# Dealing the rows of a weight matrix to partitions in groups of four, and reading the other matrix's columns with a step of four

## The chip, the cores and the metric

The kernel runs on one core of a Trainium2 chip. The metric is the device time of one execution in microseconds (us). TensorE (PE in the profile, with PEld for its weight loads), VectorE (DVE), ScalarE (ACT), GpSimd (POOL) and the DMA engines work beside each other and wait for one another through semaphores.

## The reference

A gated linear attention (4 batches, 8 heads, 768 positions, head size 48) is followed by one feed-forward block over all 3072 tokens, whose activation is a rational function:

```python
state = f[:, :, t, :, None] * state + einsum('bhd,bhe->bhde', k[:, :, t], v[:, :, t])   # f = sigmoid(f_logit)
y[:, :, t] = einsum('bhd,bhde->bhe', q[:, :, t], state)
...
x = y.transpose(0, 2, 1, 3).reshape(3072, 384)
h = x @ w_in                                   # w_in 384 x 2048
P = a[0] + a[1]*h + a[2]*h**2 + a[3]*h**3
Q = 1.0 + abs(b[0])*abs(h) + abs(b[1])*h**2
out = (P / (Q + 1e-06)) @ w_out                # w_out 2048 x 384
```

All inputs and the output are float32. The hidden dimension of 2048 is an inner one: w_in makes its columns, w_out sums over its rows, and nothing else depends on the order in which its 2048 elements are kept.

## The kernel before, in words

The 3072 tokens are worked off in 12 units of 256 tokens (one batch and 256 positions each). A unit has an attention part, which ends in `xT`, the 384 features of its 256 tokens in bf16, three blocks of 128 on the partitions, and a feed-forward part. The 2048 hidden elements are cut into 16 tiles of 128, which lie on the partitions. Both weight matrices stay in SBUF in bf16 for the whole run: `w_in_sb` is 128 partitions x 3 feature blocks x 2048 columns, `w_out_sb` is 128 partitions x 16 hidden tiles x 384 columns.

The steps that matter here:

- `wi m0 m1` (L199) loads the columns of w_in for the hidden tiles m0 to m1, `wo m0 m1` (L205) the rows of w_out for them. Each is called four times with four tiles at a time. They are issued on GpSimd's DMA queue and convert float32 to bf16 on the way.
- `h n m0 m1` (L454) makes the hidden tiles m0 to m1 of unit n: for each tile three matmuls, one per feature block, with 128 columns of `w_in_sb` as the weights that are loaded into the array and the 256 columns of `xT` streamed past them, into the PSUM tile `hp`. `ha` and `hb` (L478) do the same for one group of unit 0 in two halves. Together they are 12 units x 16 tiles x 3 = 576 matmuls, each with a weight load of its own, in 48 groups of four tiles.
- `hy` (ACT, L484) copies `hp` to bf16. `sq`, `ab`, `p1`, `p2`, `pm`, `tv`, `gm` on DVE, `ln`, `lz`, `ex` on ACT, `u` on PE (L505) and the adding DMAs `zd` and `ta` on POOL (L519, L549) make the activation `gall` from it.
- `o n j m0 m1` (L567) sums the output of 128 tokens over the hidden tiles: `gall` is the loaded weight, the 384 columns of a tile of `w_out_sb` are streamed, into `op`. There are 384 of these matmuls. `oe` copies `op` out of PSUM, `so` stores it.
- On the attention side, `T` (L320) transposes, `sc` (L345) makes scores, `yb` and `yi` (L367) outputs, `kv` (L414, L420) and `si` (L425) states, `vm` (POOL, L360) copies part of v.

The order of all of these is a table written out by hand (`ORDER`); each engine carries out its own steps in that order and waits only for data and for buffers. Four PSUM slots pass between the PE steps. In the table the steps on w_out stand as follows:

```
... xa 3 0; wo 8 12; ...            wo 12 16; dz 1 @2; h 2 8 12 @2
... vm 3 1; wo 4 8; hy 2 8 12; wo 0 4; ...
o 0 1 8 12 @2; ...  o 0 0 8 12; ... o 0 1 12 16; ... o 0 1 4 8; ... o 0 1 0 4; ...
```

Of the kernel before, what the change touches and what calls it, by code (L numbers as in the profile page):

```python
# [100 lines left out]
def _at(t, dims, off=0):  # L101

    return bass.AP(tensor=t.tensor, offset=t.offset + off, ap=[t.ap[0]] + [list(d) for d in dims])
# [3 lines left out]
def kernel(  # L107
# [12 lines left out]
    nc = tc.nc  # L120
    B, H, S, D = q.shape
    C = 128
    P = 128
# [8 lines left out]
    R = C // 2  # L132
    E = 64
    W = 2 * D

    nc.scalar.preload_act_table_set("natural_log_exp_and_others")

# [19 lines left out]
    vmp = [consts.tile([P, 2, HP, 48], BF16, name=f"vmp{i}") for i in range(2)]  # L157
    states = [[consts.tile([P, HP, W], BF16, name=f"state{b}_{j}") for j in range(UB)] for b in range(B)]
    a_sb = consts.tile([P, 4], F32, name="a_sb")
# [5 lines left out]
    w_in_sb = consts.tile([P, KD, d_ff], BF16, name="w_in_sb")  # L165
    w_out_sb = consts.tile([P, KF, DM], BF16, name="w_out_sb")
# [5 lines left out]
    def unit(n):  # L172
        if n not in units:
            c, b = divmod(n, B)
            units[n] = dict(c=c, b=b, qk=qkp[n % 2], ls=lsp[n % 2], vm=vmp[n % 2], st=states[b])
        return units[n]

    def slot(i, shape, dtype, name):
        return slots[i].tile(shape, dtype, name=name, tag="s")
# [22 lines left out]
            behind(i, hold[1:])  # L202

    def load_w_out(m0, m1, hold=None):
        i = nc.gpsimd.dma_start(out=w_out_sb[:, m0:m1, :],  # L205
                            in_=moe_w_out[m0 * P:m1 * P, :].rearrange("(ko ki) n -> ki ko n", ki=P))
        if hold is not None:
            behind(i, hold[1:])

# [21 lines left out]
    def const_z(i):  # L231
        if i < 2:
            nc.vector.memset(lsp[i][:, :, :, D:E], 0.0)
            nc.vector.memset(qkp[i].rearrange("p i x h d -> p (i x h) d")[:, :, D:E], 0.0)
            nc.vector.memset(vmp[i][:, :, :, 16:32], 0.0)
        elif i == 2:
            nc.vector.memset(ind, 0.0)
            for j in range(UB):
                nc.vector.memset(ind[R * j:R * j + R, j:j + 1], 1.0)
        else:  # L240
            for b in range(B):
                nc.vector.memset(states[b][0].rearrange("p a d -> p (a d)").bitcast(F32), 0.0)
# [155 lines left out]
    def sv_open(n, sl):  # L398
        s = unit(n)
        if "sv" not in s:  # L400
            t = s["svt"] = slot(sl, [P, UB, 512], F32, "sv")
            s["sv"] = t[:, :, 0:HP * W].rearrange("p j (a e) -> p j a e", a=HP)
            s["al"] = t[:, 0, 448:448 + 2 * HP].rearrange("p (a j) -> p a j", j=UB)
# [39 lines left out]
    def st(n, j):  # L443
        s = unit(n)
        return nc.vector.tensor_mul(s["st"][1 - j], s["sv"][:, j], _at(s["ae"], [[UB, HP], [0, W]], j))

    def h(n, m0, m1, sl):
        s = unit(n)  # L450
        t = s["hp", m0] = slot(sl, [P, 4, NT], F32, "hp")
        for m in range(m0, m1):
            for kk in range(KD):
                nc.tensor.matmul(t[:, m - m0, :], w_in_sb[:, kk, m * P:(m + 1) * P],  # L454
                                 s["x"][:, kk].rearrange("p i j t -> p (i j t)"),
                                 start=(kk == 0), stop=(kk == KD - 1))

# [8 lines left out]
    def ha(n, m0, m1, sl):  # L466
        s = unit(n)
        s["hp", m0] = slot(sl, [P, 4, NT], F32, "hp")
        hk(n, m0, m1, 0)

    def hb(n, m0, m1):
        for kk in range(1, KD):
            hk(n, m0, m1, kk)

    def hk(n, m0, m1, kk):
        s = unit(n)
        for m in range(m0, m1):
            nc.tensor.matmul(s["hp", m0][:, m - m0, :], w_in_sb[:, kk, m * P:(m + 1) * P],  # L478
                             s["x"][:, kk].rearrange("p i j t -> p (i j t)"),
                             start=(kk == 0 and (m - m0) % 2 == 0), stop=(kk == KD - 1), skip_group_check=True)  # L480

# [100 lines left out]
    def behind(i, mark):  # L582
        tc.add_manual_dep(i.ins, marks[mark].ins.name,
                          mybir.DependencyInfo(mybir.DependencyClass.Sync, mybir.DependencyReason.DATA),
                          reason="begins behind it")

    steps = dict(ld=load, wi=load_w_in, wo=load_w_out, ab_=load_ab, cu=const_u, ci=const_i, cm=const_m,
                 cz=const_z, fa=coef_a, fb=coef_b, fr=coef_r, ef=ef, ls=ls, cs=cs, A=A, xa=xa, T=T, Te=Te,
                 sc=sc, mk=mk, vm=vm, yi=yi, yb=yb, kv=kv, si=si, ye=ye, ae=ae, st=st, h=h, ha=ha, hb=hb, hy=hy, sq=sq, ab=ab, u=u, ln=ln,
                 zv=zv, zd=zd, sa=sa, lz=lz, ex=ex, p1=p1, p2=p2, pm=pm, ta=ta, tv=tv, gm=gm, o=o, oe=oe, so=store, dz=dz)  # L590
    for step in ORDER.replace("\n", ";").split(";"):
# [34 lines left out]
```

## Time and profile before

| | |
|---|---|
| Time, median of 3 runs | 216.9 us (216.26 to 217.07) |
| Span of the profiled execution | 214.4 us |
| Median less span | 2.5 us |
| Busy: PE / DVE / ACT / POOL | 201.0 / 201.7 / 195.8 / 83.7 us |
| Granted TensorE clock | 1.000 |
| DMA | 43.20 MB in 61199 packets, mean 202 GB/s |

The span runs from the first to the last instruction of the execution that the profiler recorded. That execution's time outside the profiler is not listed beside it, so the 2.5 us around the span are taken from the median of the runs. [...] "Idle before" is the time an engine stood still ahead of an instruction, with what ended it.

### The profile page before, as it was taken

What the parts mean: (1) busy time and instruction counts of PE and PEld (TensorE: products, weight loads), DVE (VectorE), ACT (ScalarE), POOL (GpSimd) and SP (SyncE); (2) the same over time, 40 slices, a digit from 0 to 9 for tenths busy, and PEclk for the clock granted to TensorE, in tenths of its full rate; (3) what the DMA queues carried; (4) which work ended last, traced back from release to release, by engine and by line L of the source; (5) the groups of instructions that cost most, each with busy time, mean ns of one, the idle gap of its engine ahead of it and who ended that gap; (6) DMA issues with size and microseconds to landing.
All of it is one profiled execution on the core that took longest, in us unless ns stands there. A gap on an engine that the chain in (4) does not pass through costs nothing.

```text
span 214.4 us, 7128 instructions
## 1 busy us (share of the span) xinstructions
PE 201.0 (94%) x3166; PEld 139.9 (65%) x3166; DVE 201.7 (94%) x213; ACT 195.8 (91%) x204; POOL 83.7 (39%) x93
## 2 busy tenths in 40 slices
PE   5875999899999999999999899999999999999993
PEld 1544587567767686586687587686577676776461
DVE  4786899999999999999999999999999999999991
ACT  3574689999999999999999999999999999999990
POOL 5161009009165072183270496696350603114200
PEclk9999999999999999999999999999999999999999
DMA  5999999999999999999999499999499896988823
GB/s 143 240 257 217 201 242 197 195 223 223 187 200 248 247 235 219 253 228 203 192 292 193 81 294 215 209 225 208 89 192 200 164 196 126 174 282 151 187 84 148
DMA packets 61199, 43.20 MB, mean 202 GB/s; under 512 B 51184, under 2 KB 55024, under 8 KB 61168
## 3 DMA queue, kind: packets, MB, share of 16 engines
q0 software_dynamic: 21520, 23.86, 67.3%
q1 hardware_dynamic: 39360, 18.68, 34.5%
q8 instruction: 25, 0.41, 0.8%
q10 hardware_dynamic: 288, 0.20, 0.3%
q14 instruction: 6, 0.05, 0.1%
HBM read 25.17 MB, written 4.72 MB: 139 GB/s over the span
## 4 chain that ended last, share of the span: by engine, by line
PE 39%; DVE 29%; ACT 14%; DMA 9%; issue 6%; SPq 2%; POOL 1%; DVEq 0%
PE hp L454 13%; PE op L567 12%; DVE gall L557 6%; DMA w_in_sb<-in_moe_w_in_dram 6%; DVE gall L545 4%; ACT qi L527 4%; ACT hy L484 4%; DVE z L497 3%; DVE h L489 3%; DVE scm L353 3%; DMA fn<-in_f_logit_dram 3%; PE u L505 3%; DVE gall L531 3%; PE y L367 2%; DVE hy L536 2%
## 5 line engine op out<-in xcount | busy, mean ns | idle before, releaser
L567 PE MATMUL op<-w_out_sb,gall 128*128 128x384 bf16 x384 | 69.2, 326 | 0.4 <-DVE gall L557 0.4
L454 PE MATMUL hp<-xT,w_in_sb 128*128 128x256 bf16 x564 | 66.7, 273 | 2.1 <-DMA w_in_sb<-in_moe_w_in_dram 2.0
L454 PEld LDWEIGHTS <-w_in_sb 128*128 128x128 bf16 x564 | 54.2, 98 | 11.5 <-DMA w_in_sb<-in_moe_w_in_dram 2.5
L567 PEld LDWEIGHTS <-gall 128*128 128x128 bf16 x384 | 36.1, 98 | 23.6 <-DVE gall L557 0.8
L484 ACT CAST hy<-hp 128x1024 bf16<-128x1024 f32 x47 | 48.1, 1076 | 2.3 <-PE hp L478 1.4
L527 ACT ACTIVATE qi<-lq 128x2048 bf16<-128x2048 f32 (+1 forms) x26 | 48.0, 1861 | 0.1
L360 POOL COPY vmp<-vn 128x128 bf16<-128x128 bf16 x24 | 35.2, 1516 | 28.4 <-DMA vn<-in_v_dram 22.7
L549 POOL DMA_DIRECT2D gall<-hy x20 | 20.0, 1068 | 53.9 <-ACT lsp L276 10.6
L523 ACT ACTIVATE lq<-z 128x2048 f32<-128x2048 bf16 (+1 forms) x20 | 36.8, 1874 | 0.0
L353 DVE TENSOR_TENSOR scm<-sc,mask 128x1024 bf16<-128x1024 f32 x24 | 29.0, 1215 | 1.9 <-PE sc L345 1.7
L489 DVE TENSOR_TENSOR h<-hy 128x4096 bf16<-128x4096 bf16 (+2 forms) x19 | 28.5, 1500 | 0.0
L557 DVE TENSOR_TENSOR gall<-gall,qi 128x4096 bf16<-128x4096 bf16 (+2 forms) x17 | 28.2, 1666 | 0.2
L545 DVE TENSOR_TENSOR gall<-gall,h 128x4096 bf16<-128x4096 bf16 (+2 forms) x17 | 28.1, 1652 | 0.0
L519 POOL DMA_DIRECT2D z<-h x17 | 19.3, 1366 | 17.0 <-PE u L505 6.0
L302 ACT ACTIVATE A<-cs 128x768 f32<-128x768 f32 (+1 forms) x26 | 19.4, 799 | 1.8 <-PE cs L286 1.8
L193 POOL DMA_DIRECT2D vn<-in_v_dram x12 | 12.4, 1030 | 15.7 <-PE y L367 7.9
L531 DVE TENSOR_SCALAR gall<-hy,a_sb 128x4096 bf16<-128x4096 bf16 (+1 forms) x14 | 16.9, 1208 | 0.0
L536 DVE TENSOR_SCALAR hy<-hy,a_sb 128x4096 bf16<-128x4096 bf16 (+1 forms) x14 | 16.6, 1185 | 0.0
L497 DVE TENSOR_SCALAR z<-hy 128x4096 uint16<-128x4096 uint16 (+2 forms) x19 | 15.7, 834 | 0.4 <-ACT hy L484 0.4
L330 ACT COPY qkT<-tp 128x1024 f32<-128x1024 f32 x11 | 11.6, 1058 | 3.2 <-PE tp L320 3.2
L320 PE MATMUL tp<-ident,qkp 128*128 128x128 bf16 x192 | 12.9, 219 | 0.8 <-DVE qkp L308 0.5
L320 PEld LDWEIGHTS <-qkp 128*128 128x128 bf16 x192 | 11.5, 98 | 2.5 <-DVE qkp L308 0.9
(73 smaller groups left out, 255.8 us busy)
## 6 DMA issues: line engine op xcount, KB each, us to landing
gall<-hy POOLq DMA_DIRECT2D x18, 512.0 KB, 7.1
z<-h POOLq DMA_DIRECT2D x15, 512.0 KB, 8.4
fn<-in_f_logit_dram SPq DMA_DIRECT2D x11, 384.0 KB, 8.5
kn<-in_k_dram SPq DMA_DIRECT2D x11, 384.0 KB, 12.1
qn<-in_q_dram SPq DMA_DIRECT2D x11, 384.0 KB, 11.3
out_dram<-osb SPq DMA_DIRECT2D x11, 384.0 KB, 5.1
vn<-in_v_dram POOLq DMA_DIRECT2D x12, 192.0 KB, 8.9
w_in_sb<-in_moe_w_in_dram POOLq DMA_DIRECT2D x4, 384.0 KB, 10.1
```

The source lines that it names most:

```text
L320: nc.tensor.transpose(t[:, x, i, p, :], s["qk"][:, i, x, 2 * p:2 * p + 2, :].rearrange("t h d -> t (h d)"), ident)
L353: return nc.vector.tensor_mul(t, s["sc", g].rearrange("s r a i t -> s (r a) (i t)"), mb)
L360: nc.gpsimd.tensor_copy(s["vm"][:, :, :, 32 * x:32 * x + 16], src)
L454: nc.tensor.matmul(t[:, m - m0, :], w_in_sb[:, kk, m * P:(m + 1) * P], s["x"][:, kk].rearrange("p i j t -> p (i j t)"), start=(kk == 0), s ...
L484: (nc.scalar.copy if eng == "s" else nc.vector.tensor_copy)(fl(big(s, "hy", "hy", 3), m0, m1), fl(s["hp", m0], 0, m1 - m0))
L489: return nc.vector.tensor_mul(fl(big(s, "h2", "h2", 2), m0, m1), fl(s["hy"], m0, m1), fl(s["hy"], m0, m1))
L523: nc.scalar.activation(fl(lq, m0, m1), fl(s["z"], m0, m1), AF.Ln, scale=regs[2], bias=1.0 + 1e-6)
L527: nc.scalar.activation(fl(qi, m0, m1), fl(lq, m0, m1), AF.Exp, scale=-1.0)
L531: return nc.vector.tensor_scalar(fl(big(s, "g", "gall", 3), m0, m1), fl(s["hy"], m0, m1), a_sb[:, 3:4], a_sb[:, 2:3], op0=ALU.mult, op1=AL ...
L545: return nc.vector.tensor_mul(fl(s["g"], m0, m1), fl(s["g"], m0, m1), fl(s["h2"], m0, m1))
L557: return nc.vector.tensor_mul(fl(s["g"], m0, m1), fl(s["g"], m0, m1), fl(qi, m0, m1))
L567: nc.tensor.matmul(s["op", j][:, j, 0:DM], s["g"][:, m, P * j:P * j + P], w_out_sb[:, m, :], start=(s["on", j] == 1), stop=(s["on", j] == KF))
```

## The change

In the hidden dimension, each group of 512 elements was kept as four tiles of 128 neighbours: element 128 m + p of w_out's rows lay in partition p of tile m. Now partition p holds the four neighbouring elements 4p to 4p + 3 of the group, one in each of the group's four tiles. For the load of w_out that makes a partition's part of a call one run of four rows (6144 B of float32 in DRAM, 3072 B of bf16 in SBUF) in place of four runs of one row (1536 B and 768 B). For the hidden tiles to hold the same elements, the weights of a matmul of `h` are every fourth of 512 columns of `w_in_sb` in place of 128 neighbouring columns; the load of w_in itself and its place in SBUF are as they were.

```diff
+    RW = 4
...
     def load_w_out(m0, m1, hold=None):
-        i = nc.gpsimd.dma_start(out=w_out_sb[:, m0:m1, :],
-                            in_=moe_w_out[m0 * P:m1 * P, :].rearrange("(ko ki) n -> ki ko n", ki=P))
+        i = nc.gpsimd.dma_start(out=w_out_sb[:, m0:m1, :].rearrange("k (g r) n -> k g (r n)", r=RW),
+                            in_=moe_w_out[m0 * P:m1 * P, :].rearrange("(g k r) n -> k g (r n)", k=P, r=RW))
...
+    def wcols(kk, m):
+        g, r = divmod(m, RW)
+        return w_in_sb[:, kk, g * RW * P:(g + 1) * RW * P].rearrange("k (p r) -> k p r", r=RW)[:, :, r]
+
     def h(n, m0, m1, sl):
...
-                nc.tensor.matmul(t[:, m - m0, :], w_in_sb[:, kk, m * P:(m + 1) * P],
+                nc.tensor.matmul(t[:, m - m0, :], wcols(kk, m),
                                  s["x"][:, kk].rearrange("p i j t -> p (i j t)"),
...
     def hk(n, m0, m1, kk):
...
-            nc.tensor.matmul(s["hp", m0][:, m - m0, :], w_in_sb[:, kk, m * P:(m + 1) * P],
+            nc.tensor.matmul(s["hp", m0][:, m - m0, :], wcols(kk, m),
```

No instruction is added, removed or moved on any engine. On GpSimd the four loads of w_out stand where they stood and change their shape; before:

```order
L549 DMA gall<-hy 128x2048
L360 COPY vmp_94<-vn 128x8x16
L205 DMA w_out_sb<-in_moe_w_out_dram 128x4x384
L549 DMA gall<-hy 128x2048
L205 DMA w_out_sb<-in_moe_w_out_dram 128x4x384
L193 DMA vn<-in_v_dram 128x8x96
```

And after, with the line numbers of the changed kernel:

```order
L554 DMA gall<-hy 128x2048
L361 COPY vmp_94<-vn 128x8x16
L206 DMA w_out_sb<-in_moe_w_out_dram 128x1536
L554 DMA gall<-hy 128x2048
L206 DMA w_out_sb<-in_moe_w_out_dram 128x1536
L194 DMA vn<-in_v_dram 128x8x96
```

The neighbours are the same; what was four rows of 384 per partition is one run of 1536 elements. On TensorE the 6334 rows are the same in both kernels but for line numbers.

## The prediction

> **What bounds the kernel now.** I read the page first, then the chain of waits in order of time, then who waited for whom, and last the groups of weight loads.
>
> ```profile
> PE 201.0 (94%) x3166; PEld 139.9 (65%) x3166; DVE 201.7 (94%) x213; ACT 195.8 (91%) x204; POOL 83.7 (39%) x93
> PE   5875999899999999999999899999999999999993
> PE 39%; DVE 29%; ACT 14%; DMA 9%; issue 6%; SPq 2%; POOL 1%; DVEq 0%
> ```
>
> The three compute engines are full, and PE carries the largest share of the chain that ended last. Busy time alone doesn't say whether PE has slack, so the question goes to its waits, from the point where the weights are in (27 us) to the end. The columns are: who waited, for whom, us in total, times, longest.
>
> ```profile
> PE y L367 <- DVE scm L353: 1.0, 1, 1.0
> PE cs L286 <- ACT hy L484: 0.6, 1, 0.6
> PE op L567 <- DVE gall L557: 0.4, 1, 0.4
> PE tp L320 <- ACT xT L436: 0.3, 1, 0.3
> PE hp L454 <- DMA w_in_sb<-in_moe_w_in_dram: 0.3, 1, 0.3
> ```
>
> That is 2.6 us of listed waiting in 187 us, and none of it is for w_out. PE therefore has next to no slack: time added to its stream is time added to the end, and time that a DMA saves has almost nothing to give back. How the stream of PE runs is seen in a stretch of the chain (start, us, what):
>
> ```profile
> 58.48 2.62 PE hp L454 x24
> 61.10 0.65 PE op L567 x4
> 61.75 0.37 PE sv L414 x32
> 62.12 0.28 PE sv L420 x8
> ...
> 64.75 2.62 PE hp L454 x24
> 67.38 0.65 PE op L567 x4
> 68.03 0.39 PE sc L345 x16
> 68.41 0.76 PE op L567 x4
> ```
>
> Matmul follows matmul without a hole. A matmul of `h` takes 2.62 / 24 = 109 ns of the stream, one of `o` 163 ns. The 8 matmuls of L420 stream only 2 columns each and load 128 columns of weights each, and one of them takes 0.28 / 8 = 35 ns.
>
> **The load of w_out.** Four DMAs of 128 x 4 = 512 runs each become four of 128 runs.
>
> ```profile
> L205 POOL DMA_DIRECT2D w_out_sb<-in_moe_w_out_dram x4 | 3.3, 834 | 0.0
> w_out_sb<-in_moe_w_out_dram POOLq DMA_DIRECT2D x4, 384.0 KB, 12.6
> w_in_sb<-in_moe_w_in_dram POOLq DMA_DIRECT2D x4, 384.0 KB, 10.1
> L205 POOL DMA_DIRECT2D w_out_sb<-in_moe_w_out_dram x4: 756/760/1060, 37.1 to 52.2; - x4
> DMA to landing us min/median/max: 8.8/12.6/14.3
> 48.48 0.86 POOL L549 DMA_DIRECT2D gall<-hy  x1 [10.60 <-ACT lsp L276]
> ```
>
> The issue costs POOL 4 x 834 ns = 3.3 us. With a quarter of the runs it can fall by anything from 0 to 3.3 us. What it frees is worth nothing by itself, since POOL is busy 39% of the span and stood still for 10.6 us right behind the first of these loads.
>
> The landing has a nearest row: w_in moves the same bytes in 384 runs and lands in 10.1 us against 12.6 us. I take 10 to 12.6 us for the new landing. The first user sets what that is worth. By the table of steps the groups of `o` come in the order of hidden tiles 8-12, 8-12, 12-16, 4-8, 0-4. In the chain these are the groups at 61.10, then two up to 64.75, then 67.38 and 68.41. The last load (tiles 0-4) is issued at 52.2 us and lands by 52.2 + 14.3 = 66.5 us at the latest, 1.9 us ahead of its first use. So a faster landing gives 0. If a landing became slower by more than 1.9 us, PE would wait for the rest; a load with longer runs and the same bytes has no row that speaks for that. I book 0.
>
> Other transfers could land sooner as well, since all share the same DMA engines. PE's list above has no wait for a load of f, k, q or v after 27 us. Booked at 0, with the 2.6 us of waits as the most that any indirect relief could remove.
>
> **The weight loads of `h`.** This is the only edit that touches the full engine. All 576 keep their number, place and size, and their columns lie 8 B apart where they lay 2 B apart. The streamed operand `xT` and the PSUM side are untouched. No weight load with a step stands in the trace, so its cost must be bounded from rows with neighbouring columns:
>
> ```profile
> L454 PEld LDWEIGHTS <-w_in_sb 128*128 128x128 bf16 x564 | 54.2, 98 | 11.5 <-DMA w_in_sb<-in_moe_w_in_dram 2.5 <-issue 0.3
> L367 PEld LDWEIGHTS <-vn 64*32 64x32 bf16 x384 | 7.8, 90 | 4.7 <-issue 3.6
> L414 PEld LDWEIGHTS <-qkp 64*64 64x64 bf16 x384 | 4.2, 109 | 2.1 <-issue 1.1 <-DMA vn<-in_v_dram 0.6 <-DVE qkp L308 0.2
> ```
>
> The cover first. A load runs while the matmul ahead of it streams. L420 shows a full load of 128 columns followed by a matmul every 35 ns, so a load needs at most 35 ns of the stream. Inside a group of `h` each load has 109 ns. The difference, 109 - 35 = 74 ns, is how much longer a load may take before any matmul is late: up to 98 + 74 = 172 ns in this view.
>
> Below nothing: excluded inside the groups. The loads are already covered, so a shorter one moves nothing.
>
> Above: 32 columns take 90 ns and 64 take 109 ns, so these smaller loads pay 19 ns for each further 32 columns, 0.6 ns a column. The loads of 128 columns, at 98 ns, are shorter than those of 64: the full-width load has a quicker form. The lowest bound is that the step changes nothing: 98 ns, cost 0. The middle one is that the quicker form is lost: 109 + 2 x 19 = 147 ns, 49 ns more, still under the 74 ns of cover. The upper one is that each column also costs twice as much as in those rows: 71 + 4 x 38 = 223 ns, 125 ns more, of which 51 ns are bare; 576 x 51 ns = 29.4 us.
>
> I take the lowest. The nearest row is that of the same load with the same 128 rows and columns, and even the middle bound stays under cover inside a group.
>
> [...]
>
> **The sum.** 0 for the landing, 0 for POOL, 0 for DVE and ACT (same instructions, same data sizes), 0 for PE. The span stays at 214.4 us, which with the 2.5 us around it is 216.9 us. I put the forecast at 216.8 us, a tenth under it, for the little that fewer runs may give the queues.
>
> **The rivals.**
>
> Second case, loads slower but under the cover. The loads in the middle of a group stay hidden; the first load of a group is covered only by what stands ahead of it. In PE's order 33 groups or pairs of groups of `h` follow something else; 20 of them stand behind matmuls of 384 or 512 streamed columns, 7 behind `sc`, 3 behind `T`, 2 behind L420 and 1 behind L367. The chain shows what a bare first load costs now:
>
> ```profile
> 75.46 2.62 PE hp L454 x24
> 78.08 0.35 PE sc L345 x16
> 78.43 2.73 PE hp L454 x24
> ```
>
> Behind `sc` the same 24 matmuls take 0.11 us more. If each of the 13 short-covered starts pays the middle bound, 13 x 49 ns = 0.6 us; at the full 74 ns of cover, 13 x 74 ns = 1.0 us. That gives 217.5 to 217.9 us, hardly to be told from no change. For it: the quicker form could be tied to neighbouring columns. Against it: nothing in the trace. [...]
>
> Third case, loads past the cover, slower than before. From 172 ns on, every one of the 576 matmuls waits for its weights. At 223 ns it is 51 ns each. PE has no waits to absorb it: 216.9 + 29.4 = 246 us. Between the point of 172 ns and 223 ns lies all from 218 to 246 us; the middle is 232 us. For it: the load reads four times as wide a stretch of SBUF, 1024 B instead of 256 B in each partition, at a rate that neighbouring columns never asked for. Against it: a load would have to grow to 1.75 times its length. [...]
>
> Fourth case, faster. The loads of w_out free POOL and the DMA engines, and a transfer on which others wait comes sooner:
>
> ```profile
> POOL vmp L360 <- DMA vn<-in_v_dram: 22.7, 4, 8.0
> ```
>
> POOL waits long for v, and its copies feed L367 on PE. But PE's own waits name no copy of v, so at most the 2.6 us listed can go: 214.3 to 215.8 us. The loads of w_out touch only the stretch from 37 to 67 us, where the only listed wait of PE is the 1.0 us for `scm`, which POOL does not make.
>
> **How the numbers follow.** No change 0.58, second case 0.12, third 0.22, fourth 0.08. Half a per cent, 1.1 us, is about what a measurement can tell here. Of the second case a quarter may end over that bound (0.03). So slower is 0.22 + 0.03 = 0.25, faster 0.08, same 0.67. The range takes in the first two cases (0.70, 216 to 218 us), most of the fourth down to 215.0 us (0.06) and the low end of the third, up to 223 us, where a load has grown to 182 ns and each matmul is 10 ns late (576 x 10 ns = 6 us), about 0.05: 0.81 in all. The likeliest case's own range is 216.0 to 217.9 us.
>
> **What would show it.** Right: the group of weight loads of `w_in_sb` stays near 98 ns, 24 matmuls of `h` still take 2.62 us in the chain, w_out lands in 10 to 12.6 us, and nobody waits for it. Second case: loads of some 147 ns, 2.62 us inside a group and over 2.73 us behind `sc`. Third case: matmuls of `h` further apart than 109 ns throughout, PE's share of the chain well over 39%, DVE and ACT waiting for `hp`. Wrong altogether: PE waiting for `w_out_sb` near 61 or 68 us, or the span changing with the matmuls of `h` still 109 ns apart.

## The result, and the profile after

The changed kernel takes 229.43 us (median of 4 runs, 229.23 to 229.6) against 216.69 us before: a ratio of 1.0588, 95% interval 1.0559 to 1.0617. The ratios here and below are estimated from the runs in the chip's fast state, so they need not be the quotient of the medians beside them. The forecast was 216.8 us, with a range up to 223. The profiled execution took 229.6 us with a span of 227.9 us, 13.5 us more than before.

The page of the changed kernel, engines, slices of 5.7 us and the chain:

```profile
PE 202.0 (89%) x3158; PEld 147.3 (65%) x3166; DVE 201.8 (89%) x213; ACT 195.5 (86%) x204; POOL 83.9 (37%) x93
PE   5770068998999999999999999999999999999994
DVE  4782027999999999999999999999999999999991
PEclk9997559999999999999999999999999999999999
PE 37%; DVE 30%; ACT 13%; DMA 9%; issue 6%; SPq 1%; POOL 1%; DVEq 0%
```

The busy times of the compute engines are within 1 us of those of before; PEld, the weight loads, is 7.4 us longer. What is new is a hole: PE shows 0 in the fourth and fifth slice, DVE falls with it, and the granted clock goes to half (5 tenths in the fifth and sixth slice). Behind it the slices are full again.

The weight loads of `h`, on which the prediction spent most of its working, are a little longer and still covered. Groups of weight loads, then the stretch of the chain that answers to the one shown before:

```profile
L459 PEld LDWEIGHTS <-w_in_sb 128*128 128x128 bf16 x564 | 61.3, 114 | 18.4 <-issue 15.0
```

```profile
71.98 2.62 PE hp L459 x24
74.60 0.65 PE op L572 x4
75.25 0.37 PE sv L415 x32
75.62 0.28 PE sv L421 x8
```

A load takes 114 ns in place of 98, and 24 matmuls of `h` take the same 2.62 us, 109 ns each. The loads of w_out land in 9.7 us in place of 12.6, and no wait for them shows among PE's:

```profile
w_out_sb<-in_moe_w_out_dram POOLq DMA_DIRECT2D x4, 384.0 KB, 9.7
```

Most of that is not the work of the longer runs. In the second experiment below the loads keep their old shape and are only issued later, and they land in 9.9 us; with the new shape and the timing of before they take 11.5 to 11.7 us.

The time went in one place. PE's timeline around the first matmuls of `h`, before (start, us, what, idle before it and what ended that):

```profile
16.81 1.48 PE L454 MATMUL hp<-xT,w_in_sb 128*128 128x256 bf16 x12 [1.74 <-DMA w_in_sb<-in_moe_w_in_dram]
21.08 0.61 PE L478 MATMUL hp<-xT,w_in_sb 128*128 128x256 bf16 x4 [1.90 <-DMA w_in_sb<-in_moe_w_in_dram]
```

and after:

```profile
30.15 2.72 PE L459 MATMUL hp<-xT,w_in_sb 128*128 128x256 bf16 x12 [14.51 <-DMA w_in_sb<-in_moe_w_in_dram]
35.14 0.60 PE L483 MATMUL hp<-xT,w_in_sb 128*128 128x256 bf16 x4 [1.10 <-ACT qkT L331]
```

The first matmul of `h` starts 13.3 us later, after a wait of 14.5 us for w_in. Of the 13.3 us, 0.6 lie ahead of the wait (PE reached it at 15.6 us, before at 15.1). Which load it waits for is in the built program: a weight load names the semaphores it waits on, and each load of w_in counts on one of its own (DMASW1, 2, 4 and 5, in the order in which they are issued). Before, all waits of `h` on these:

```
L454 LDWEIGHTS w_in_sb [waits DMASW1_49]
L478 LDWEIGHTS w_in_sb [waits DMASW2_49]
L454 LDWEIGHTS w_in_sb [waits PE_49,DMASW4_49]
L454 LDWEIGHTS w_in_sb [waits DMASW5_49]
```

After:

```
L459 LDWEIGHTS w_in_sb [waits DMASW5_49,DMASW4_49,DMASW1_49]
L459 LDWEIGHTS w_in_sb [waits DMASW2_49]
```

Before, each group of hidden tiles waited for its own load of w_in. Now the first two weight loads of the first group wait for all four. The data don't ask for it: the 512 columns of a group still come with one load. But the columns are named with a step, and a load of w_in fills three separate pieces of each partition's row, one in each feature block; between these two patterns the builder that sets the waits did not find the stretches apart. The list fits a comparison by first and last element alone. Counted in a partition's row of 3 x 2048 columns, the four loads, in the order in which they are issued, reach from 1024 to 5631, 1536 to 6143, 512 to 5119 and 0 to 4607. The first weight load reads from 1024 to 1532, which lies within the first, third and fourth of these (DMASW1, 4 and 5); the second reads from 3072 to 3580, which lies within the second (DMASW2) as well. That the builder compares in this way is inferred from the list and shown by nothing else.

The sum of the stretch: 13.3 us of later start; 12 matmuls of `h` in 2.72 us instead of 1.31 and 16 of `T` in 1.19 instead of 0.92 in the chain, at a granted clock of 0.52 in the mean from 30 to 33.5 us, 1.7 us; a new wait of 1.1 us for `qkT`; less the later waits of before for w_in, 1.9 and 0.3 us, which are gone. 13.3 + 1.7 + 1.1 - 2.2 = 13.9 us, against 13.5 us of span; the 0.4 us between them are not assigned.

### The profile page after: what moved, and what is told of

Its sections match the earlier page's. It is cut to its first block, busy times and chain, and to the rows that moved or that the text cites. A ratio compares the mean times of both kernels' runs of the same rounds, so it can differ in the third digit from the quotient of the medians.

```text
span 227.9 us, 7120 instructions
## 1 busy us (share of the span) xinstructions
PE 202.0 (89%) x3158; PEld 147.3 (65%) x3166; DVE 201.8 (89%) x213; ACT 195.5 (86%) x204; POOL 83.9 (37%) x93
## 4 chain that ended last, share of the span: by engine, by line
PE 37%; DVE 30%; ACT 13%; DMA 9%; issue 6%; SPq 1%; POOL 1%; DVEq 0%
PE hp L459 12%; PE op L572 11%; DMA w_in_sb<-in_moe_w_in_dram 6%; DVE gall L562 6%; DVE gall L550 4%; DVE h L494 4%; ACT qi L532 4%; DVE z L502 4%; DVE gall L536 3%; DVE scm L354 3%; DMA fn<-in_f_logit_dram 3%; ACT hy L489 3%; PE u L510 3%; PE tp L321 3%; DVE hy L541 2%
## 5 line engine op out<-in xcount | busy, mean ns | idle before, releaser
L459 PE MATMUL hp<-xT,w_in_sb 128*128 128x256 bf16 x564 | 68.1, 276 | 14.6 <-DMA w_in_sb<-in_moe_w_in_dram 14.5
L459 PEld LDWEIGHTS <-w_in_sb 128*128 128x128 bf16 x564 | 61.3, 114 | 18.4 <-issue 15.0
L489 ACT CAST hy<-hp 128x1024 bf16<-128x1024 f32 x47 | 47.6, 1066 | 1.2 <-PE hp L483 0.6
L361 POOL COPY vmp<-vn 128x128 bf16<-128x128 bf16 x24 | 35.9, 1543 | 27.2 <-DMA vn<-in_v_dram 21.8
L489 DVE CAST hy<-hp 128x1024 bf16<-128x1024 f32 x1 | 1.2, 1225 | 14.6 <-PE hp L459 14.6
L321 PE MATMUL tp<-ident,qkp 128*128 128x128 bf16 x192 | 13.4, 222 | 0.9 <-DVE qkp L309 0.5
```

The source lines that it names most:

```text
L361: nc.gpsimd.tensor_copy(s["vm"][:, :, :, 32 * x:32 * x + 16], src)
L459: nc.tensor.matmul(t[:, m - m0, :], wcols(kk, m), s["x"][:, kk].rearrange("p i j t -> p (i j t)"), start=(kk == 0), stop=(kk == KD - 1))
L489: (nc.scalar.copy if eng == "s" else nc.vector.tensor_copy)(fl(big(s, "hy", "hy", 3), m0, m1), fl(s["hp", m0], 0, m1 - m0))
```

## The experiments

Three theories. **Wait theory**: the first matmul of `h` waits for all four loads. **Read theory** (the prediction's third case): the stepped weight loads cost it. **Landing theory**: the longer runs of w_out disturb other transfers.

**The whole change, with w_in in unbroken stretches.** The step and the dealt w_out stay; only the place of w_in's groups in SBUF is another.

```diff
-    w_in_sb = consts.tile([P, KD, d_ff], BF16, name="w_in_sb")
+    w_in_sb = consts.tile([P, KF // 4, KD, 4 * P], BF16, name="w_in_sb")
...
-        i = nc.gpsimd.dma_start(out=w_in_sb[:, :, m0 * P:m1 * P],
+        i = nc.gpsimd.dma_start(out=w_in_sb[:, m0 // 4],
...
-        return w_in_sb[:, kk, g * RW * P:(g + 1) * RW * P].rearrange("k (p r) -> k p r", r=RW)[:, :, r]
+        return w_in_sb[:, g, kk].rearrange("k (p r) -> k p r", r=RW)[:, :, r]
```

> The whole change, but w_in is kept in SBUF as 128 partitions x 4 groups x 3 blocks x 512 columns, so that each of its four loads fills one unbroken stretch of a partition. The step of four and the dealt w_out stay. Wait theory (the 12.7 us are the first matmul of h waiting for all four loads of w_in instead of the first): that wait falls from 14.5 us to about 2 us, the first matmul of h starts near 17 us instead of 30.1, and the time comes back to 216.7 us within 0.5 us. Read theory (the stepped weight loads, 114 ns for 98 ns, cost it): the loads keep their step, so the time stays near 229 us. Landing theory (w_out's longer runs disturb other loads): stays near 229 us too.

Measured: 216.77 us against 216.72, ratio 0.9995 (0.9964 to 1.0026). The four waits of the built program are those of before, one load each. PE's timeline and its weight loads:

```profile
17.88 1.50 PE L459 MATMUL hp<-xT,w_in_sb 128*128 128x256 bf16 x12 [2.01 <-DMA w_in_sb<-in_moe_w_in_dram]
L459 PEld LDWEIGHTS <-w_in_sb 128*128 128x128 bf16 x564 | 60.8, 113 | 5.7 <-DMA w_in_sb<-in_moe_w_in_dram 2.7 <-issue 0.3
```

The loads have their step and their 113 ns, and the loss is gone. Read and landing theory fall.

**The wait alone, put into the kernel before.**

```diff
+                if n == 0 and m0 == 8 and m == 8 and kk == 0:
+                    for mark in ("wi.12.16", "wi.4.8", "wi.0.4"):
+                        behind(i, mark)
```

> The kernel before, with neighbouring columns and w_out as it was, but the first matmul of h is made to wait for all four loads of w_in. Wait theory: slower by all of the 12.7 us, 229.4 us within 0.7 us, with a half-speed TensorE clock in the stretch of the wait as in the changed kernel. Read theory: no step, so 216.7 us. Landing theory: 216.7 us.

Measured: 230.17 us against 216.72, ratio 1.0595 (1.055 to 1.0641), as in the changed kernel (1.0588), though just past the 0.7 us that the expectation allowed. In the chain `T` takes 1.72 us in place of 1.19 here, where the half-speed clock lasted longer (17.07 us against 13.65). The same picture, without any step:

```profile
30.72 2.72 PE L455 MATMUL hp<-xT,w_in_sb 128*128 128x256 bf16 x12 [14.64 <-DMA w_in_sb<-in_moe_w_in_dram]
L455 PEld LDWEIGHTS <-w_in_sb 128*128 128x128 bf16 x564 | 54.9, 99 | 24.4 <-issue 15.2
```

With the run above, the wait is shown to be the cause from both sides: taking it out of the change removes the loss, putting it into the kernel before makes it.

**The dealt w_out alone**, on the kernel before:

```diff
-        i = nc.gpsimd.dma_start(out=w_out_sb[:, m0:m1, :],
-                            in_=moe_w_out[m0 * P:m1 * P, :].rearrange("(ko ki) n -> ki ko n", ki=P))
+        i = nc.gpsimd.dma_start(out=w_out_sb[:, m0:m1, :].rearrange("k (g r) n -> k g (r n)", r=RW),
+                            in_=moe_w_out[m0 * P:m1 * P, :].rearrange("(g k r) n -> k g (r n)", k=P, r=RW))
```

> The kernel before with the load of w_out alone dealt in groups of four; w_in's columns are read as before, so hidden elements are multiplied with rows of w_out that aren't theirs. Wait theory: 216.7 us within 0.5 us, since no load of w_in is waited for differently; the landing of w_out falls from 12.6 to 9 to 11 us and nobody waited for it. Landing theory: slower by up to 12.7 us. Read theory: 216.7 us.

Measured: 216.99 us against 216.72, ratio 1.0004 (0.9981 to 1.0027). The landing was 11.7 us here, less of a gain than expected; it is worth nothing either way.

**The step alone**: the first experiment with the load of w_out as before (the diff above, reversed).

> The step of four alone, with w_in's groups in unbroken stretches and the load of w_out as before; hidden elements are multiplied with rows of w_out that aren't theirs. Wait theory: 216.7 us within 0.5 us, weight loads of w_in at 114 ns and matmuls of h still 109 ns apart, because 16 ns more lie under 74 ns of cover. Read theory: near 229 us. The difference from the kernel with both edits and unbroken stretches is what w_out's load is worth: expected 0 to 0.3 us.

Measured: 216.72 us against 216.72, ratio 0.9991 (0.9966 to 1.0016), loads of 113 ns, and in the chain:

```profile
58.25 2.62 PE hp L459 x24
64.52 2.62 PE hp L459 x24
```

So, with w_in in unbroken stretches, the step is worth nothing that can be measured, and so are both edits together; the dealt w_out alone is worth nothing in the old layout.

**Other steps.** How far is a stepped load from the end of its cover? In the last kernel the 128 columns were taken from a flat view of the group's three blocks with other steps.

```diff
-        return w_in_sb[:, g, kk].rearrange("k (p r) -> k p r", r=RW)[:, :, r]
+        flat = w_in_sb[:, m // 4].rearrange("k b c -> k (b c)")
+        return flat[:, o:o + 127 * step + 1:step]
```

> Unbroken stretches for w_in, w_out as before, weight columns read with a step of two (4 B); the columns are not the right ones, so h is not the reference's. [...] Step theory (the cost grows with the step, 5 ns each): 103 ns. [...]

> The same with a step of eight (16 B); wrong columns, so h is not the reference's. [...] Step theory: 98 + 7 x 5 = 133 ns. By both it stays under the cover that ends at 172 ns: matmuls of h 109 ns apart, 216.7 us within 0.5 us. The third case of the prediction (a load past the cover) would show here first: over 172 ns, matmuls further apart, several us slower.

> The same with a step of twelve (24 B); wrong columns, so h is not the reference's. [...] Step theory: 98 + 11 x 5 = 153 ns. Both under 172 ns: 216.7 us within 0.5 us. A load past the cover would spread the matmuls of h beyond 109 ns and cost several us.

Measured, as the weight loads of `w_in_sb` in the three traces (shortest, median, longest in ns), steps two, eight and twelve:

```profile
L460 PEld LDWEIGHTS <-w_in_sb x564: 96/98/100, 15.4 to 195.4; 128*128 128x128 bf16 x188
```

```profile
L460 PEld LDWEIGHTS <-w_in_sb x564: 140/143/170, 16.7 to 193.8; 128*128 128x128 bf16 x188
```

```profile
L460 PEld LDWEIGHTS <-w_in_sb x564: 137/143/170, 17.9 to 194.9; 128*128 128x128 bf16 x188
```

Steps one, two, four, eight and twelve take 98, 98, 113, 143 and 143 ns. Step theory falls: two costs no more than one, and twelve no more than eight. From two to four the load grew by 15 ns, from four to eight by 30 ns. What sets these times isn't shown. None passes the cover, though the longest loads, 170 ns, come near the 172 that the prediction worked out for it. With step eight the chain has

```profile
64.90 2.62 PE hp L460 x24
```

and the time is 217.09 us against 216.92 (0.9974 to 1.0044); with step twelve 217.39 us (1.0004 to 1.0064, so perhaps 0.3% slower). The one run with step two took 217.97 us, and no interval stands behind it.

What a longer load does cost is seen where the cover is short. The prediction showed 24 matmuls of `h` behind `sc`, 2.73 us where they take 2.62 inside the stream. At the same place the chains of step four (the step alone), eight and twelve have

```profile
78.19 2.75 PE hp L459 x24
78.60 2.77 PE hp L460 x24
79.64 2.78 PE hp L460 x24
```

That is 0.02, 0.04 and 0.05 us more, for loads that are 15, 45 and 45 ns longer. Over the 13 short-covered starts that the prediction counted, it would make 0.3 to 0.7 us, an estimate from this one start; the intervals of steps eight and twelve hold it.

**Waiting for two loads**: the kernel with the wait alone, with only `"wi.12.16"` in its list.

> The kernel before with the first matmul of h waiting for the first two loads of w_in instead of the first alone. By the trace of before the second load is there at about 20.9 us, so the first matmul of h moves from 16.8 to 20.9 us, 4.1 us. The 1.9 us that PE waited for the same load later, ahead of L478, go. If the price of the wait is the delay of what stands behind it in PE's order, the time rises by 4.1 - 1.9 = 2.2 us to 218.9 us; if the later wait for the third load (until 26.8 us, 0.3 us) takes that up, it stays within 0.5 us of 216.7. The full wait costs 12.7 us in either case.

Measured: 221.29 us against 216.53, ratio 1.0243 (1.0165 to 1.0322): slower, though four runs don't settle whether by 2%. The expectation of 218.9 us was too low by 2.4 us. The trace has the start where it was expected and what was left out behind it:

```profile
21.18 2.72 PE L455 MATMUL hp<-xT,w_in_sb 128*128 128x256 bf16 x12 [6.03 <-DMA w_in_sb<-in_moe_w_in_dram]
23.69 1.91 PE L321 MATMUL tp<-ident,qkp 128*128 128x128 bf16 x16
26.71 0.60 PE L482 MATMUL hp<-xT,w_in_sb 128*128 128x256 bf16 x4 [1.10 <-ACT qkT L331]
```

4.4 us of later start, 1.4 us for 12 matmuls of `h` at half clock (2.72 instead of 1.31 us), 0.8 us for `T` (1.72 instead of 0.92 us in the chain), 1.1 us for the new wait, less 2.2 us of waits that are gone: 5.5 us, against 4.8 us measured. The clock was at half behind this wait of 6.03 us as well: 0.76 in the mean from 16 to 30 us.

**Filling the wait**, on the changed kernel, with warming matmuls ahead of the first group of `h`:

```diff
-wi 0 4; h 0 8 12 @1;
+wi 0 4; dz 55 @0; h 0 8 12 @1;
```

> The changed kernel with 55 warming matmuls of 512 columns (55 x 216 ns = 11.9 us, into a scratch PSUM tile) in PE's order just ahead of the first matmul of h, so that PE is busy while it would wait for the four loads. The wait for the loads stays, its end stays near 30 us. If the whole loss is the wait, the time stays at 229.4 us. If the half-speed clock behind the wait takes part, the 12 matmuls of h go back from 2.72 to 1.31 us and the 16 of T from 1.19 to 0.92 us, and the time falls by 1.4 + 0.3 = 1.7 us to 227.7 us.

Measured: 230.37 us, four runs from 228.12 to 233.2, ratio to before 1.0542 (1.0503 to 1.0581). With that spread the 1.7 us can't be told. The filling ended early, PE stood still for another 3.5 us, and the clock fell all the same, to 0.52 in the mean from 30 to 33.5 us:

```profile
30.46 2.72 PE L459 MATMUL hp<-xT,w_in_sb 128*128 128x256 bf16 x12 [3.51 <-DMA w_in_sb<-in_moe_w_in_dram]
```

So 72 of them:

> The changed kernel with 72 warming matmuls in place of 55 in the wait. The 55 ended 3.5 us ahead of the last load of w_in, and the clock fell to half all the same. 72 x 216 ns = 15.6 us reach past the landing at 30 us, so PE is still busy when the loads are there. If the half-speed clock takes part in the loss, the 12 matmuls of h behind the wait take 1.31 us instead of 2.72 and those of T 0.92 instead of 1.19; the filling may end up to 1.5 us after the landing, which is taken off again. 228 to 229.5 us against 229.4; if h's 12 matmuls take 1.31 us, the clock's part is shown whatever the sum.

Measured: 230.31 us, ratio 1.0619 (1.0562 to 1.0676), past the 228 to 229.5 that were expected. The chain, in order of time:

```profile
15.81 15.54 PE warm L296 x72
31.35 1.31 PE hp L459 x12
32.66 0.91 PE tp L321 x16
33.56 0.02 issue
33.59 1.02 ACT qkT L331
```

The clock's part of the stretch is shown here: at a granted clock of 1.00 from 16 to 44 us `h` takes 1.31 us and `T` 0.91 us, and `qkT` starts at 33.59 us, against 34.08 us in the changed kernel, although `h` began 1.2 us later. The whole did not gain, and not all of that is explained. In both filled kernels PE stands still once, for 1.6 and 1.7 us, for nothing that the profile shows, near 166 us in the first one and near 118 us in the second. The kernel with step two, which isn't filled, has such a stop of 1.0 us as well, and the other kernels have none at this line. The second filled kernel, then that of step two:

```profile
PE y L368 <- issue: 1.7, 1, 1.7
PE y L368 <- issue: 1.0, 1, 1.0
```

So the stop need not come from the filling; what brings it stays open. That the wait makes the loss rests on the first two experiments; how much of the 12.7 us the fallen clock adds to it at the end isn't shown.

## Why the prediction was wrong

- **Where it failed: in its list of waits, in the term "0 for PE".** The step "All 576 keep their number, place and size" costed the weight loads only by their duration. In its place the runs showed a wait: the first matmul of `h` stood 14.5 us for all four loads of w_in where it had stood 1.7 us for one, and the time rose by 12.7 us. It looked for what the edit of w_in's columns adds as time of an instruction and not as a condition for its start. That all instructions keep their order was read as the waits keeping theirs; the semaphores that each weight load waits on were not compared, though they were to be had before any run. The rival "slower" was priced at 218 to 246 us by another mechanism, loads past the cover. That the measured 229.4 us lies inside is luck: the loads stayed under the cover.
- **The loads of `h`**: cost 0, right. They lie at 114 ns, between the bound of nothing (98) and the middle one (147), under the 172 ns estimated as the end of the cover; the matmuls stayed at 109 ns. The second case is there in kind and too small to be told in the time: at 16 ns more, 13 starts make 0.2 us, and the one start shown above was 0.02 us later.
- **The load of w_out**: worth 0, right. It landed in 9.7 us where 10 to 12.6 was expected, still ahead of its first use; with the timing of before it was 11.5 to 11.7, inside the range.
- **PE has no slack**: right, and it is what made the wait dear. 13.3 us of later start came out as 13.5 us of span, since no engine behind it had room to catch up. (The 2.5 us around the span were the median less the span of one execution; the profiled execution of the changed kernel has 1.7.)
- **What it named as a sign of being wrong altogether**, the span changing with matmuls 109 ns apart, is what happened; it named w_out as the thing waited for, and it was w_in.

## What to carry to other kernels

When an access pattern changes, compare what each instruction waits for, and not only the order and the duration: a slice with a step may be seen by the builder as meeting loads of its tile that it has nothing to do with, and then waits for them too. The semaphores that an instruction waits on stand in the built program, before any run. A load that fills one unbroken stretch of a partition kept such slices apart at no cost here (ratio 0.9995). Where the bounding engine has next to no slack, count a wait at the start as time at the end: here 13.3 us of later start came out as 13.5 us of span, and the granted clock was at half for 13.65 us, from inside the wait until 3 us behind it.

## What the runs showed of the hardware

- A weight load of 128 bf16 columns took 98, 98, 113, 143 and 143 ns at steps of one, two, four, eight and twelve elements. Inside a group none of it reached the matmuls of 256 columns, 109 ns apart; a group behind `sc` ended 0.02 to 0.05 us later.
- PE's granted clock fell to half while PE stood still ahead of `h`, or right behind that. Ahead of the end the traces record one stretch at half: 13.65 us in the changed kernel (19.7 to 33.3 us), 17.07 us with the wait put into the kernel before, 6.83 us with the wait for two loads and 3.41 us in the first filled kernel, which are four, five, two and one times 3.41 us (the mean granted clocks of these executions are 0.97, 0.963, 0.984 and 0.993). What sets these lengths isn't shown. In the changed kernel the clock was 0.63 in the mean from 16 to 30 us and 0.52 in the 3.5 us behind (stretch, its length, then PE, PEld, DVE, ACT and POOL busy with counts, granted clock, DMA share, GB/s):

```profile
16.00:30.00 14.00, 0.00 (x0) 0.00 (x0) 2.24 (x5) 0.55 (x1) 2.12 (x4) 0.63 1.30 213
30.00:33.50 3.50, 3.35 (x22) 2.60 (x23) 0.59 (x1) 0.00 (x0) 0.26 (x1) 0.52 1.04 231
```

- Behind a stop of 3.5 us (the first filled kernel) came one stretch of 3.41 us, and behind shorter ones too, at times: with a step of twelve PE stood still for 1.7 us ahead of `h`, and one stretch at half clock followed, here with the 3.41 us ahead of it. The kernel with the dealt w_out alone has one behind a stop of 1.9 us, that with step two behind 2.1 us; the first experiment's kernel stopped for 2.0 us and has none. What decides between these isn't shown.

```profile
14.75:18.16 3.41, 1.69 (x80) 1.21 (x80) 2.77 (x5) 2.11 (x3) 3.30 (x5) 1.00 1.04 195
18.16:21.58 3.42, 3.42 (x24) 2.95 (x23) 1.63 (x5) 0.00 (x0) 0.00 (x0) 0.50 1.29 202
```
